# The head of a fused conv and gate kernel: the first superblock's scatters moved ahead of most loads of the second, scatters shared out anew between SP and POOL, one eviction on VectorE, one block's order, six more zero matmuls

## The chip, the core and the metric

The kernel runs on one core of a Trainium2 chip. The metric is the time that the device takes for one execution, in microseconds (us), as the median over runs.

## What is computed

Two stages on x of shape (8, 4224, 192), cut to what matters. First a causal convolution over time with 7 taps, whose taps are a softmax per head (8 heads of 24 channels); then a gated projection.

```python
w = softmax(weight, axis=-1)                    # (8 heads, 7 taps)
a[b, s, h, :] = sum_k w[h, k] * x_pad[b, s + k, h, :]
gate_pre[b, s, :] = sum_k conv_w[k, :] * a_pad[b, s + k, :]   # 5 taps
gate = sigmoid(gate_pre)
out = (gate * (a @ w_val)) @ w_out              # both 192 x 192
```

All of it is float32.

## The kernel before

**Layout.** The eight sequences lie as two streams of four, back to back, with padding between. The streams are cut into 14 *superblocks*; superblock g has NJS[g] windows of 122 tokens for each of 5 strips of a head (2, 3, 3, 3, then 5). The 192 channels fill one and a half times 128 partitions, so a superblock of `a` is held as x1 (128 partitions: heads 0 to 4 and a third of head 5, both streams beside each other) and x2 (the other 64 channels, one stream on each half of the partitions).

**First stage.** The convolution of the first stage is a matmul (line 312): 128 tokens of a window on the partitions, 120 columns (5 strips x 24 channels) as the stationary operand, and a 128 x 122 band matrix made of the softmax weights as the moving one. Four such matmuls fill a PSUM tile `pc_u`; that is a *unit* u. Superblock 0 has units 0 to 3, superblock 1 units 4 to 9, superblock 2 units 10 to 15, superblock 3 units 16 to 21. Heads come in the order 6, 7, 5, 0, 1, 2, 3, 4 (QUADS). In float32 each matmul stands as two records in the profile. ScalarE copies the unit's PSUM tile to SBUF (line 321, tile `e`). When all windows of a head are copied, `scatter` (lines 333 to 363) issues DMAs that move its rows from `e` to their partitions in x1 or x2: one DMA for heads 0 to 4, two for heads 6 and 7, four for head 5. These DMAs are issued by SP, except that in superblocks 0 to 2 heads 5, 6 and 7 are issued by POOL (but two of head 5's DMAs in superblock 0), and heads 3 and 4 of superblock 0 by ScalarE.

**Loads.** x arrives by DMAs from SP, `x_i` (line 161), with two heads in each for superblocks 0 to 3: x_0 to x_3 are superblock 0, x_4 to x_7 superblock 1, x_8 to x_11 superblock 2. There are eight buffers. Six loads and the weights (`wv`, `wo`) are issued at the start (lines 188 to 192); the later ones are issued from `conv_unit` once a load's last head has been scattered, up to the number that `allowed` (line 143) gives. SP's queue is in order: a scatter that waits for its eviction holds up each load behind it.

**Second stage.** It runs over *blocks* n, two for superblocks 0 to 3 (blocks 0 and 1 are superblock 0). For the 5-tap gate, ScalarE opens an accumulator in PSUM (`pa` for the x1 part, `pb` for x2, line 384), VectorE adds the other four taps (line 391) and ScalarE closes it with a sigmoid into g1 or g2 (line 404). The projection splits each float32 operand into two parts, h rounded by ScalarE (lines 412, 420) and l = x - h by POOL (lines 413, 421), and makes three matmuls of each product (`diagonal`, `main`, `rows`, lines 447 to 470); a smaller piece goes in plain float32 (`columns`, line 485). The 192 output channels come as three chunks, 0 and 1 (the two streams of the first 128) and 2. VectorE multiplies value and gate (line 504, into g), the product is split again and projected with w_out, ScalarE copies the result out (line 520) and SP stores it (line 525).

**Order.** No scheduler reorders anything: each engine executes in the order in which the code is written. The prologue (lines 548 to 569) decodes the weights on VectorE, does the units 0 to 9 and opens blocks 0 and 1; the loop at line 571 does blocks 0 to 3, the loop at line 604 the rest. WARM (line 94) are counts of matmuls on zeros (line 204), which compute nothing that is used: 11 ahead of unit 0, 5 ahead of unit 4, 14 ahead of unit 7.

In the profile's rows and below, buffer numbers are left out where a group is meant: `x<-xw` is a load, `x<-e` a scatter, `pc<-band,x` a unit's matmul, `pw<-zero` a zero matmul.

Of the kernel before, what the change touches and what calls it, by code (L numbers as in the profile page):

```python
# [22 lines left out]
M = NS * HC  # L23
# [69 lines left out]
BY_POOL, EARLY, AHEAD = 3, 4, 6  # L93
WARM = 11, 5, 14

# [6 lines left out]
def kernel(  # L102
# [40 lines left out]
    def allowed(i):  # L143
        g = loads[i][0]
        a, b = first_load[g], first_load[g + 1]
        if g == 0:
            return b + 2 if i < b - 1 else first_load[2]
        if g == 1:
            return b + (0, 2, 2, 4)[i - a]
        if g < EARLY:  # L150
            return b + (first_load[g + 2] - b) * (i + 1 - a) // (b - a)
        return i + 1 + AHEAD
# [34 lines left out]

    load_x(3)
    load_raw("wv")
    load_x(4)  # L190
    load_raw("wo")
    load_x(6)

# [104 lines left out]
    def conv_unit(u):  # L298
# [21 lines left out]
        w = len(ws) * WIN  # L320
        nc.scalar.copy(e[:, a : a + w], pc[:M, :w])  # L321
        done = [hi for hi, j in ws if j == n - 1]
        for hi in done:
            h = QUADS[q][hi]
            i, at = home[g, h]
            last = at == len(loads[i][1]) - 1
            if last and g >= BY_POOL:
# [5 lines left out]
    def scatter(g, h, e):  # L333
# [3 lines left out]
        x1, x2 = x1s[g], x2s[g]  # L337
        if g < BY_POOL and h >= 5:
            dma = nc.gpsimd.dma_start
        elif g == 0 and h in (3, 4):  # L340
            dma = nc.scalar.dma_start
        else:
            dma = nc.sync.dma_start
# [10 lines left out]
        else:  # L354
# [4 lines left out]
            for i, (a, b) in enumerate(ends):  # L359
                if h == 5:  # L360
                    send(x2[64 * i + 48 : 64 * i + 64], 8, HC, a, b, nc.sync.dma_start if g == 0 else dma)
                else:
                    send(x2[64 * i + h - 6 : 64 * i + 48 : 2], 0, HC, a, b)
# [126 lines left out]
    def split(n):  # L490
        if n >= N:
            return
        x1, x2 = views(n)
        if n == 0:
            xs[n, 2] = split2(sp, "x", n, x2)
        xs[n, 1] = split1(sp, "x", n, x1)
        if n > 0:
            xs[n, 2] = split2(sp, "x", n, x2)
# [48 lines left out]

    nc.scalar.activation(warm2, rs[:, 0:1], AF.Sigmoid)
    w_val.decode()
    w_val.join(nc.vector)  # L550
    put(cwt.rearrange("p a k -> p (a k)"), w_val.pr, 0, 128, 2 * D, 2 * D + 2 * KG)
    conv(first_unit[1])
    w_val.cast(nc.gpsimd)
# [17 lines left out]
    for n in range(HEAD):  # L571
        k = 2 if n < 2 else 3
        diagonal("v", n)
        split(n + 1)
        diagonal("o", n - 1)
        main("v", n, 0)
        main("v", n, 1)
        gate_taps(n + 1, 0, 1, k)
        columns("v", n)
# [143 lines left out]
```

## Time and profile before

| what | value |
|---|---|
| median of 3 runs | 390.54 us (390.15 to 391.44) |
| the profiled execution | 393.35 us, of which its span 391.6 us |
| TensorE busy | 378.0 us (97%) |
| VectorE busy | 342.3 us (87%) |
| ScalarE busy | 323.8 us (83%) |
| GpSimd busy | 254.8 us (65%) |
| DMA | 82.49 MB, 211 GB/s on average |
| granted TensorE clock, mean | 0.991 |

Times in the profile count from the start of the span. PE is TensorE, PEld its weight load, DVE is VectorE, ACT is ScalarE, POOL is GpSimd, SP is SyncE; a q behind a name is that engine's DMA queue, where the row's duration is that of the issue and not of the transfer. A row of the timeline gives the start, the duration from the first to the last of a merged group, the instruction, and in brackets the idle time of the engine just before it with what ended it. The chain of waits is followed back from the last instruction, at each step to what released it. A row of the stretches gives busy time and count for PE, PEld, DVE, ACT and POOL, then the granted clock, the share of the 16 DMA engines that was busy, and GB/s.

### The profile page before, as it was taken

How to read it: one execution, taken by the hardware profiler on the slowest of the kernel's cores; microseconds unless marked ns; L12 is line 12 of the kernel's file. 1: busy time of each engine (PE TensorE's matmuls, PEld its weight loads, DVE VectorE, ACT ScalarE, POOL GpSimd, SP SyncE). 2: the span in 40 equal slices, each digit the busy share in tenths (PEclk: the TensorE clock that was granted, in tenths of full speed). 3: DMA queues.
4: the chain of work that ended last, by engine and by line, in shares of the span. 5: the costliest groups of instructions: out<-in, count | busy, mean ns of one | idle time of the engine just before them, and what ended most of it. 6: DMA issues, size and time to landing. Idle time of an engine off the chain costs nothing.

```text
span 391.6 us, 8620 instructions
## 1 busy us (share of the span) xinstructions
PE 378.0 (97%) x3204; PEld 321.6 (82%) x3204; DVE 342.3 (87%) x424; ACT 323.8 (83%) x525; POOL 254.8 (65%) x177
## 2 busy tenths in 40 slices
PE   8699999999999999999999999999999999999895
PEld 8687988898888888888888888888888787788684
DVE  4669899888998998998999899899899999999970
ACT  7458888988888888888889988888888888887863
POOL 1959765566667665666665666766566676776871
PEclk9969999999999999999999999999999999999999
DMA  8777869998687689778868868758987644333223
GB/s 293 210 195 223 253 214 290 258 239 272 210 251 216 180 260 256 210 217 253 224 194 256 219 185 261 218 178 253 257 226 227 211 160 146 114 135 133 80 106 144
DMA packets 38209, 82.49 MB, mean 211 GB/s; under 512 B 4856, under 2 KB 17528, under 8 KB 38168
## 3 DMA queue, kind: packets, MB, share of 16 engines
q1 hardware_dynamic: 36720, 79.90, 67.6%
q0 software_dynamic: 896, 1.31, 1.4%
q10 hardware_dynamic: 552, 0.73, 0.6%
q8 instruction: 25, 0.41, 0.5%
q14 instruction: 16, 0.13, 0.1%
HBM read 29.34 MB, written 26.00 MB: 141 GB/s over the span
## 4 chain that ended last, share of the span: by engine, by line
PE 72%; DVE 13%; DMA 5%; ACT 4%; issue 3%; SPq 2%; POOL 0%; DVEq 0%; ACTq 0%
PE pc L312 20%; PE o L457 10%; PE v L457 9%; PE v L485 7%; PE v L470 6%; PE o L485 6%; DVE pa L391 6%; PE o L470 5%; PE o L447 5%; PE v L447 4%; DVE pb L391 4%; DVE g L504 3%; DMA x<-e 2%; DMA x<-xw 2%; DMA scr<-wv 1%
## 5 line engine op out<-in xcount | busy, mean ns | idle before, releaser
L391 DVE SCALAR_TENSOR_TENSOR pa<-x,cwt,pa 128x1004 f32<-128x1004 f32 (+5 forms) x144 | 172.9, 1201 | 10.7 <-ACT pa L384 6.8
L413 POOL TENSOR_TENSOR xl<-x,xh 128x1004 fp32r<-128x1004 f32 (+5 forms) x36 | 74.8, 2077 | 73.1 <-ACT xh L412 58.9
L312 PEld LDWEIGHTS pc<-band,x 128*120 128x120 f32 x912 | 103.1, 187 | 7.1 <-issue 3.9
L312 PE MATMUL pc<-band,x 128*120 128x122 f32 x912 | 104.2, 272 | 4.3 <-DMA x<-xw 3.8
L391 DVE SCALAR_TENSOR_TENSOR pb<-x,cwt,pb 128x502 f32<-128x502 f32 (+5 forms) x144 | 102.2, 710 | 3.8
L413 POOL TENSOR_TENSOR pl<-g,ph 128x1004 fp32r<-128x1004 f32 (+5 forms) x36 | 79.4, 2204 | 10.3 <-ACT ph L412 7.7
L504 DVE TENSOR_TENSOR g<-v,g 128x502 f32<-128x502 f32 (+5 forms) x108 | 65.8, 642 | 21.1 <-PE v L470 16.1
L404 ACT ACTIVATE g<-pa 128x1004 f32<-128x1004 f32 (+5 forms) x36 | 34.5, 959 | 38.8 <-DVE pa L391 21.1
L321 ACT COPY e<-pc 120x488 f32<-120x488 f32 x114 | 59.1, 586 | 6.4 <-PE pc L312 6.3
L421 POOL TENSOR_TENSOR pl<-g,ph 128x502 fp32r<-128x502 f32 (+5 forms) x36 | 43.0, 1194 | 32.8 <-ACT ph L420 32.7
L520 ACT COPY ot<-o 128x502 f32<-128x502 f32 (+5 forms) x108 | 56.2, 551 | 3.3 <-PE o L457 2.6
L421 POOL TENSOR_TENSOR xl<-x,xh 128x502 fp32r<-128x502 f32 (+5 forms) x36 | 41.8, 1162 | 0.0
L384 ACT ACTIVATE pa<-x,cwt 128x1004 f32<-128x1004 f32 (+5 forms) x36 | 37.8, 1051 | 4.8 <-DMA x<-e 3.7
L485 PEld LDWEIGHTS v<-x,wvf 128*64 128x64 f32 x576 | 29.1, 136 | 11.8 <-issue 11.4
L485 PE MATMUL v<-x,wvf 128*64 128x125 f32 (+4 forms) x576 | 37.2, 270 | 0.0
L412 ACT CAST ph<-g 128x1004 fp32r<-128x1004 f32 (+5 forms) x36 | 35.1, 976 | 1.5 <-DVE g L504 1.5
L485 PE MATMUL o<-g,wof 128*64 128x125 f32 (+4 forms) x576 | 35.6, 264 | 0.0
L412 ACT CAST xh<-x 128x1004 fp32r<-128x1004 f32 (+5 forms) x36 | 34.6, 961 | 0.0
L485 PEld LDWEIGHTS o<-g,wof 128*64 128x64 f32 x576 | 30.9, 136 | 0.1
L457 PE MATMUL o<-ph,woh 128*128 128x502 f32 (+5 forms) x72 | 30.9, 429 | 0.0
L457 PE MATMUL v<-xh,wvh 128*128 128x502 f32 (+5 forms) x72 | 27.2, 377 | 0.3 <-ACT e L321 0.3
L457 PE MATMUL v<-xh,wvl 128*128 128x502 f32 (+5 forms) x72 | 27.1, 377 | 0.0
(75 smaller groups left out, 573.1 us busy)
## 6 DMA issues: line engine op xcount, KB each, us to landing
x<-xw SPq DMA_DIRECT2D x64, 300.0 KB
out<-ot SPq DMA_DIRECT2D x24, 753.0 KB
x<-e SPq DMA_DIRECT2D x40, 285.9 KB
x<-xw SPq DMA_DIRECT2D x20, 360.0 KB
out<-ot SPq DMA_DIRECT2D x8, 672.0 KB
x<-e SPq DMA_DIRECT2D x32, 141.6 KB
x<-e SPq DMA_DIRECT2D x25, 171.6 KB
x<-e SPq DMA_DIRECT2D x16, 94.4 KB
```

The source lines that it names most:

```text
L312: nc.tensor.matmul(pc[:M, k * WIN : (k + 1) * WIN], lhsT=xtiles[i][:, c : c + M], rhs=band[:, 4 * q + hi, :], start=True, stop=True,)
L321: nc.scalar.copy(e[:, a : a + w], pc[:M, :w])
L384: nc.scalar.mul(acc, views(n, 0)[i], cwt[:, i, 0:1])
L391: nc.vector.scalar_tensor_tensor(out=acc, in0=views(n, k)[i], scalar=cwt[:, i, k : k + 1], in1=acc, op0=ALU.mult, op1=ALU.add,)
L412: nc.scalar.copy(h, x)
L413: nc.gpsimd.tensor_tensor(out=l, in0=x, in1=h.bitcast(F32), op=ALU.subtract)
L421: nc.gpsimd.tensor_tensor(out=l, in0=x, in1=h.bitcast(F32), op=ALU.subtract)
L457: nc.tensor.matmul(acc, lhsT=a[:, r], rhs=b[:, q], start=(fresh and i == 0), stop=(not fresh and i == 2))
L470: nc.tensor.matmul(acc, lhsT=a[p, r], rhs=b[p], start=(fresh and i == 0), stop=(not fresh and i == 2))
L485: nc.tensor.matmul(acc[p, c], lhsT=w.f[:, W12 : W12 + 64], rhs=x[:, q, c], start=False, stop=(i == 3),)
L504: nc.vector.tensor_tensor(out=v, in0=banks.pop(("v", n, q)), in1=v, op=ALU.mult)
L520: nc.scalar.copy(ots[n][:, q * m : (q + 1) * m], banks.pop(("o", n, q)))
```

## The change

Seven things are changed, all in the head (superblocks 0 to 2):

1. The load x_3 is issued ahead of `wv`.
2. Load x_5 is no longer issued at the start, but behind the scatter of head 0 of superblock 0; x_6 and x_7 are issued behind the scatter of head 6 of superblock 1, which waits for the eviction of pc_4, and no longer behind the scatters of superblock 0.
3. The table FROM_POOL now says which heads POOL scatters: of superblock 0 heads 5, 6, 7 and, new, head 2; of superblock 1 heads 5 and 7, and no longer head 6; of superblock 2 none. SP issues the rest, and in superblock 1 also the two DMAs of head 5's rows in x2.
4. Unit 0 is evicted by VectorE instead of ScalarE, and unit 0 is written ahead of the decoding of w_val, so that VectorE has the copy ahead of that decoding.
5. In block 1 ScalarE and POOL split the x2 part (chunk 2) ahead of the x1 part.
6. In block 1 TensorE does the `diagonal` of the output projection of block 0 behind `main` of the values and no longer ahead of it.
7. 20 zero matmuls stand ahead of unit 7 instead of 14.

SP's queue in the head, before, from the fourth load to the loads of superblock 2 (x_i are loads with their numbers, scr the raw weights, x1_g and x2_g the rows of superblock g, e_g_q the evicted heads; the last number of each name only tells tiles apart):

```order
L186 DMA scr_2_101<-wv 128x788
L161 DMA x_3_105<-xw 128x480
L186 DMA scr_1_100<-wo 128x768
L161 DMA x_4_108<-xw 128x720
L161 DMA x_5_110<-xw 128x720
L350 DMA x2_0_177<-e_0_0_178 16x5x122 x2
L350 DMA x1_0_176<-e_0_0_178 24x5x244
L350 DMA x1_0_176<-e_0_1_200 24x5x244 x2
L161 DMA x_6_217<-xw 128x720
L161 DMA x_7_219<-xw 128x720
L350 DMA x1_1_236<-e_1_0_238 24x5x366
L161 DMA x_8_266<-xw 128x720
```

And the same stretch of SP's queue in the changed kernel:

```order
L188 DMA scr_2_101<-wv 128x788
L188 DMA scr_1_100<-wo 128x768
L163 DMA x_4_108<-xw 128x720
L354 DMA x2_0_164<-e_0_0_165 16x5x122 x2
L354 DMA x1_0_163<-e_0_0_165 24x5x244
L163 DMA x_5_198<-xw 128x720
L354 DMA x1_0_163<-e_0_1_200 24x5x244
L354 DMA x2_1_233<-e_1_0_234 24x5x180 x2
L163 DMA x_6_243<-xw 128x720
L163 DMA x_7_245<-xw 128x720
L354 DMA x2_1_233<-e_1_0_234 16x5x180 x2
L354 DMA x1_1_232<-e_1_0_234 24x5x366
```

Load x_5 has moved from ahead of three scatter issues to behind them, one scatter of superblock 0 has gone to POOL, two scatters of superblock 1 now stand ahead of x_6 and x_7, and x_8 stands behind two more (its row follows the last one shown).

TensorE before, from unit 4 to unit 7 (pc_u is unit u, pw the zero matmuls):

```order
L312 MATMUL pc_4_239<-band_91,x_4_108 120x122 x4
L312 MATMUL pc_5_247<-band_91,x_4_108 120x122 x2
L312 MATMUL pc_5_247<-band_91,x_5_110 120x122 x2
L312 MATMUL pc_6_255<-band_91,x_5_110 120x122 x4
L204 MATMUL pw_270<-zero_114 120x122 x14
L312 MATMUL pc_7_305<-band_91,x_6_217 120x122 x4
```

And in the changed kernel:

```order
L313 MATMUL pc_4_235<-band_91,x_4_108 120x122 x4
L313 MATMUL pc_5_247<-band_91,x_4_108 120x122 x2
L313 MATMUL pc_5_247<-band_91,x_5_198 120x122 x2
L313 MATMUL pc_6_255<-band_91,x_5_198 120x122 x4
L205 MATMUL pw_270<-zero_112 120x122 x20
L313 MATMUL pc_7_311<-band_91,x_6_243 120x122 x4
```

The order there is the same; six zero matmuls are added, six matmuls (pc_4 and half of pc_5) need x_4 alone, the six behind them x_5.

SP's queue for superblock 2 before, with the loads around it:

```order
L161 DMA x_10_327<-xw 128x720
L161 DMA x_11_329<-xw 128x720
L161 DMA x_12_410<-xw 128x720
L350 DMA x1_2_387<-e_2_0_389 24x5x366
L161 DMA x_13_423<-xw 128x720
```

And in the changed kernel:

```order
L163 DMA x_10_333<-xw 128x720
L163 DMA x_11_335<-xw 128x720
L354 DMA x2_2_394<-e_2_0_395 24x5x180 x4
L163 DMA x_12_416<-xw 128x720
L354 DMA x1_2_393<-e_2_0_395 8x5x180 x2
L354 DMA x2_2_394<-e_2_0_395 16x5x180 x2
L354 DMA x1_2_393<-e_2_0_395 24x5x366
L163 DMA x_13_429<-xw 128x720
```

Eight scatters that POOL issued now stand on SP, four of them ahead of x_12 and all of them ahead of x_13.

The diff:

```diff
--- before.py
+++ after.py
@@ -91,7 +91,9 @@
 XW = max(PER_LOAD[n] * n * M for n in NJS)
 LAG = 2
 BY_POOL, EARLY, AHEAD = 3, 4, 6
-WARM = 11, 5, 14
+
+FROM_POOL = {(0, 2), (0, 5), (0, 6), (0, 7), (1, 5), (1, 7)}
+WARM = 11, 5, 20
 
 HEAD = 4
 
@@ -144,7 +146,7 @@
         g = loads[i][0]
         a, b = first_load[g], first_load[g + 1]
         if g == 0:
-            return b + 2 if i < b - 1 else first_load[2]
+            return b + min(i + 1, 2)
         if g == 1:
             return b + (0, 2, 2, 4)[i - a]
         if g < EARLY:
@@ -185,11 +187,10 @@
     def load_raw(name):
         nc.sync.dma_start(raw[name][1], raw[name][2])
 
-    load_x(3)
+    load_x(4)
     load_raw("wv")
-    load_x(4)
     load_raw("wo")
-    load_x(6)
+    load_x(5)
 
     one = cp.tile([128, 1], F32, name="one")
     nc.vector.memset(one, 1.0)
@@ -318,12 +319,15 @@
             )
         a = (ws[0][0] * n + ws[0][1]) * WIN
         w = len(ws) * WIN
-        nc.scalar.copy(e[:, a : a + w], pc[:M, :w])
+        if u == 0:
+            nc.vector.tensor_copy(e[:, a : a + w], pc[:M, :w])
+        else:
+            nc.scalar.copy(e[:, a : a + w], pc[:M, :w])
         done = [hi for hi, j in ws if j == n - 1]
         for hi in done:
             h = QUADS[q][hi]
             i, at = home[g, h]
-            last = at == len(loads[i][1]) - 1
+            last = at == len(loads[i][1]) - 1 or (g, h) == (1, QUADS[0][0])
             if last and g >= BY_POOL:
                 load_x(allowed(i))
             scatter(g, h, e[:, hi * n * WIN : (hi + 1) * n * WIN])
@@ -335,7 +339,7 @@
         r = n * WIN
         hf = half(n)
         x1, x2 = x1s[g], x2s[g]
-        if g < BY_POOL and h >= 5:
+        if (g, h) in FROM_POOL:
             dma = nc.gpsimd.dma_start
         elif g == 0 and h in (3, 4):
             dma = nc.scalar.dma_start
@@ -358,7 +362,7 @@
                     send(x1[120:128, i * second(n) :], 0, 8, a, b)
             for i, (a, b) in enumerate(ends):
                 if h == 5:
-                    send(x2[64 * i + 48 : 64 * i + 64], 8, HC, a, b, nc.sync.dma_start if g == 0 else dma)
+                    send(x2[64 * i + 48 : 64 * i + 64], 8, HC, a, b, nc.sync.dma_start if g < 2 else dma)
                 else:
                     send(x2[64 * i + h - 6 : 64 * i + 48 : 2], 0, HC, a, b)
 
@@ -491,10 +495,10 @@
         if n >= N:
             return
         x1, x2 = views(n)
-        if n == 0:
+        if n < 2:
             xs[n, 2] = split2(sp, "x", n, x2)
         xs[n, 1] = split1(sp, "x", n, x1)
-        if n > 0:
+        if n >= 2:
             xs[n, 2] = split2(sp, "x", n, x2)
 
     def gated(n, q):
@@ -546,10 +550,11 @@
             todo[a + i * (b - a) // k] += 1
 
     nc.scalar.activation(warm2, rs[:, 0:1], AF.Sigmoid)
+    conv(1)
     w_val.decode()
     w_val.join(nc.vector)
     put(cwt.rearrange("p a k -> p (a k)"), w_val.pr, 0, 128, 2 * D, 2 * D + 2 * KG)
-    conv(first_unit[1])
+    conv(first_unit[1] - 1)
     w_val.cast(nc.gpsimd)
     w_out.decode()
     zeros(WARM[1])
@@ -572,9 +577,12 @@
         k = 2 if n < 2 else 3
         diagonal("v", n)
         split(n + 1)
-        diagonal("o", n - 1)
+        if n != 1:
+            diagonal("o", n - 1)
         main("v", n, 0)
         main("v", n, 1)
+        if n == 1:
+            diagonal("o", n - 1)
         gate_taps(n + 1, 0, 1, k)
         columns("v", n)
         gated(n, 2)
```

## The prediction

> **What bounds the kernel now.** I read the page first, then the chain of waits, then the first 40 us stretch by stretch, since the order of instructions differs only there (the first three superblocks). From the page: busy time by engine, and the chain by engine.
>
> ```profile
> PE 378.0 (97%) x3204; PEld 321.6 (82%) x3204; DVE 342.3 (87%) x424; ACT 323.8 (83%) x525; POOL 254.8 (65%) x177
> PE 72%; DVE 13%; DMA 5%; ACT 4%; issue 3%; SPq 2%; POOL 0%; DVEq 0%; ACTq 0%
> ```
>
> TensorE is busy 378.0 of 391.6 us, and the chain is 72% its work. What it loses in the head can be seen in the chain there.
>
> ```profile
> 10.70 0.89 SPq L350
> ...
> 14.35 5.89 DMA x<-xw
> 20.23 0.14 issue
> 20.37 5.22 PE pc L312 x24
> 25.59 0.02 issue
> 25.61 0.57 ACT e L321
> ...
> 28.05 0.33 ACT g L404
> 28.38 0.02 issue
> 28.40 1.24 DVE g L504 x3
> ```
>
> Read downwards: SP issues scatters; behind them in its queue stands load x_6, issued at 14.35 and landed 5.89 us later; TensorE then does pc_7 to pc_9; the last eviction, at 25.61, lets ScalarE close block 0's gates (the last from 28.05) and that releases, at 28.40, VectorE's first products. So the change is worth what it moves the end of pc_9, now 25.59, less what is lost again before 38 us.
>
> The stretches show why those matmuls are dear (after the engines' busy times come PEclk, DMA share, GB/s).
>
> ```profile
> 8.00:10.00 2.00, 2.00 (x21) 2.00 (x20) 1.90 (x6) 1.83 (x5) 0.88 (x2) 1.00 1.01 404
> 10.00:12.00 2.00, 2.00 (x21) 2.00 (x20) 1.89 (x7) 0.57 (x1) 2.00 (x4) 1.00 0.61 175
> 12.00:14.00 2.00, 2.00 (x21) 2.00 (x20) 1.88 (x6) 0.69 (x2) 1.19 (x3) 1.00 0.68 161
> 18.00:20.00 2.00, 0.00 (x0) 0.00 (x0) 1.14 (x2) 1.98 (x4) 1.98 (x5) 0.84 1.00 308
> 20.00:22.00 2.00, 1.63 (x8) 1.66 (x9) 1.93 (x3) 0.20 (x1) 2.00 (x2) 0.50 1.08 248
> 26.00:28.00 2.00, 2.00 (x26) 1.74 (x26) 0.40 (x1) 1.97 (x5) 0.00 (x0) 0.95 0.49 140
> ```
>
> And TensorE and ScalarE there, from the timeline, with the spread of landing times of all transfers of x tiles in the first 60 us.
>
> ```profile
> 6.45 3.62 PE L312 MATMUL pc<-band,x 128*120 128x122 f32 x32 [0.51 <-DVE band L229]
> 10.96 2.69 PE L312 MATMUL pc<-band,x 128*120 128x122 f32 x24
> 13.48 3.10 PE L204 MATMUL pw<-zero 128*120 128x122 f32 x28
> 20.37 5.21 PE L312 MATMUL pc<-band,x 128*120 128x122 f32 x24 [3.78 <-DMA x<-xw]
> 8.27 1.57 ACT L321 COPY e<-pc 120x488 f32<-120x488 f32 x3
> 9.31 4.99 SPq L350 DMA_DIRECT2D x<-e  x5
> 13.78 1.50 ACT L321 COPY e<-pc 120x488 f32<-120x488 f32 x3
> DMA to landing us min/median/max: 2.2/4.4/8.7
> ```
>
> Each matmul stands as two records: 12 matmuls x24. The zero matmuls end at 13.48 + 3.10 = 16.58, TensorE is idle 3.78 us, and the clock is halved within 18 to 20 (0.84 = full for 68% of it, so from 19.36, 2.8 us into the gap) and full again from about 26.2 (0.95 in 26 to 28), 5.8 us after work resumed. The same 24 records that take 2.69 us at full clock take 5.21. The stall is thus 3.8 us of waiting and 2.5 us of slow clock.
>
> **The change, part by part.** *Loads and scatters on SP.* VectorE evicts pc_0 while ScalarE does pc_1, once its matmuls are done (halfway through 3.62 from 6.45, about 8.3 to 8.4). The copy ends at about 9.0 instead of 9.3, so SP starts its scatters at 9.05, not 9.31: 0.26 earlier. Three scatters take it from 9.31 to 10.70 + 0.89 = 11.59 today, 2.28 us; load x_5, so far among the first loads, is now issued behind them, at 11.35. Its landing is the largest unknown: 2.2 to 8.7 us, median 4.4. The DMA share from 10 to 14 us is 0.61 to 0.68, against 1.00 and 1.08 from 18 to 22, when x_6 was under way, so I take 3.6, below the median: x_5 at 15.0.
>
> *TensorE.* pc_4 and the first two matmuls of pc_5 need only x_4: half of 2.69 from about 11.05, to 12.4. Then a gap that before doesn't have, 12.4 to 15.0: 2.6 us. It is just shorter than the 2.8 after which the clock fell, so I take full clock. The rest of pc_5 and pc_6 is 1.35; twenty zero matmuls are 3.10 / 14 x 20 = 4.43, of which six new ones 1.33. They end at 15.0 + 1.35 + 4.43 = 20.8.
>
> *x_6.* Its issue now waits for the eviction of pc_4, which is the first copy of the group at 13.78 and ends at about 14.35, and for the two scatters of head 6 (0.76 each by the three above): 15.9. Landing between 4.4 (median) and 5.89 (its own, with the scatters of four heads just ahead); I take 5.0: 20.9. The zeros meet it, TensorE never idles there, and pc_7 to pc_9 take 2.69: end at 23.55 instead of 25.59, a gain of 2.05.
>
> By the row above, the gap may not outlast 2.8 us. The Trainium skill, "TensorE: Matmul & The Clock Gate", section "What's actually happening", says that a free-running window of about 3.4 us decides, and that one idle window returns the clock to half. The trace agrees only in kind: 0.84 and then 0.50 follow 3.78 us of idling, the fall at 2.8. By the row the clock is safe if x_5 lands before 15.2, by the page before 15.8; at my 15.0 the sum is 2.05 by both, at 15.75 (the median) it would be 1.37 by the page and a loss by the row, which is the first rival.
>
> *Small edits, costed at nothing.* Rows that bear on them:
>
> ```profile
> 6.88 0.67 DVE L229 TENSOR_TENSOR band<-band,rs 128x488 f32<-128x488 f32 x1 [0.48 <-ACT band L221]
> 7.77 0.37 DVE L242 TENSOR_SCALAR scr<-scr 128x394 int32<-128x394 int32 x1 [0.23 <-DMA scr<-wv]
> 10.71 2.50 ACTq L350 DMA_DIRECT2D x<-e  x2
> 13.31 0.56 ACT L282 CAST wvh<-wvf 128x448 fp32r<-128x448 f32 x1 [2.63 <-DVE scr L246]
> 18.02 0.77 ACT L384 ACTIVATE pa<-x,cwt 128x608 f32<-128x608 f32 x1 [2.75 <-DMA x<-e]
> 22.27 2.26 DVE L391 SCALAR_TENSOR_TENSOR pb<-x,cwt,pb 128x304 f32<-128x304 f32 x4
> ```
>
> VectorE's copy isn't in the trace. ScalarE's takes 0.57; VectorE's products from PSUM, 304 wide, take 1.24 / 3 = 0.41, or 0.66 at 488: I take 0.6. It starts at 7.55 and ends at 8.2, where the decoding of w_val starts at 7.77 now. That decoding is late anyway: x_3 ahead of wv adds 128 x 480 x 4 B, 246 KB, which is 0.6 us at the 404 GB/s of 8 to 10 us. So wvf comes 0.7 later; ScalarE's cast of it at 13.31 stands behind DMA issues that end at 10.71 + 2.50 = 13.2, which hides it (without that cover: 0.7 on pc_4's eviction and on x_6). Head 2's scatter goes from SP to POOL, whose seventh issue it becomes. pa_0 opens when the last row of x1 lands, 18.02 now; it now also stands behind the eviction of pc_6 (16.35 + 0.6), so 17 to 18. VectorE's taps of block 0 end at 22.27 + 2.26 = 24.5, before the gate closing that would move from 28.05 to 26.0. So the gain of 2.05 reaches the products at 28.40.
>
> *Block 1 and superblock 2.* The rows:
>
> ```profile
> 31.93 0.40 PE L447 MATMUL v<-xl,wvh 128*128 128x302 f32 x1 [0.46 <-POOL xl L421]
> 32.08 2.25 DVE L391 SCALAR_TENSOR_TENSOR pb<-x,cwt,pb 128x302 f32<-128x302 f32 x4
> 34.59 1.16 DVE L391 SCALAR_TENSOR_TENSOR pa<-x,cwt,pa 128x896 f32<-128x896 f32 x1 [0.26 <-issue]
> 35.65 1.23 DVE L504 TENSOR_TENSOR g<-v,g 128x302 f32<-128x302 f32 x3
> 33.14 0.47 SPq L161 DMA_DIRECT2D x<-xw  x1
> 37.72 5.20 PE L312 MATMUL pc<-band,x 128*120 128x122 f32 x48
> 35.35 3.49 POOL L350 DMA_DIRECT2D x<-e  x6
> ```
>
> Chunk 2 first takes away the 0.46 that TensorE waits for xl of chunk 2. But from 28.40 to 36.9 VectorE is the late one: its products, taps and products follow each other with 0.26 between them, and the chain runs there. So I count 0, at most 0.46.
>
> The eight scatters of superblock 2 leave POOL (3.49 for six, 0.58 each) and stand on SP ahead of x_13, issued at 33.14 now: 33.14 - 2.05 + 8 x 0.6 = 35.9, landed at 40.3 by the median. TensorE needs x_13 at the nineteenth of the 24 matmuls from 37.72: 41.6, or 39.6 with the gain. That is 0.7 late by the median, nothing if it lands in 3.7 us; I take back 0.5. POOL's freed time buys nothing, since no row above waits for its later work.
>
> Sum: -2.05 + 0.5 = -1.55. The profiled execution took 393.35 us, its span is 391.6, so the span becomes 390.05; the median of the runs, 390.54, is 2.8 below the profiled execution, and 390.54 - 1.5 = 389.0 is the forecast.
>
> **The rivals.** *The new gap halves the clock (slower).* If x_5 lands in 4.4 us, at 15.75, the gap is 3.35 us, longer than the 2.8 that the row above needed; from 15.2 on it decides. At half clock for 5.8 us after resuming, as in before, TensorE does 2.9 us less. Between x_5's landing and the end of pc_9 stand 1.35 + 4.43 + 2.69 = 8.47, so pc_9 ends at 15.75 + 8.47 + 2.9 = 27.1, which is 1.55 late: 392.1; half of that slow time would give 390.6. For it: the median, and the scatters in the same queues. Against it: the half-empty DMA share from 10 to 14.
>
> *The gain is given back.* x_8, x_9 and x_13 all stand further back in SP's queue; if TensorE or ScalarE waits 1.5 us more for them than I take, 2.05 shrinks to nearly nothing: 390.3. For it: the landing times up to 8.7. Against it: the DMA share falls to 0.49 by 26 to 28, so there is room.
>
> *More than forecast.* x_6 lands in the median 4.4, x_13 in time and the 0.46 counts: 2.05 + 0.45, so 388.0. Against it: the zeros end only at 20.8.
>
> *Loads late, clock kept:* x_5 lands at 16.5 with a lucky phase, pc_9 ends at 25.0, less 0.5: 390.5.
>
> **How the numbers follow.** Chances: forecast 0.42 (own range 387.6 to 389.6), more than forecast 0.09, halved clock 0.27, given back 0.14, loads late 0.08. About 0.3%, 1.2 us, is what a measurement here can tell from no change: below 389.4 is faster, above 391.7 slower. Faster: 0.40 + 0.09 and 0.01 of the given-back case, 0.50. Slower: 0.20 of the halved clock, 0.03 of the late loads, 0.23. The same: 0.27. The range runs from 387.3 (a gain of 2.5 and an x_5 that lands faster still) to 392.3 (just over the halved clock's price); outside is less than 2 in 10.
>
> **What would show it.** Right: pc_5 resumes by about 15 us, the granted clock is 1.00 from 6 us on, pc_7 starts near 20.9, VectorE's first products start near 26.3, and the conv matmuls of superblock 2 run through. Wrong: a granted clock of 0.5 between 14 and 23 us, with the zero matmuls taking twice 0.22 us each; x_5 landing after 16; an idle gap of TensorE ahead of pc_17; or the first products no earlier than 28 us.

## The result and the profile after

The forecast was 389.0, faster. The changed kernel is slower, and outside the range.

| | before | after |
|---|---|---|
| median, us (lowest to highest, 6 runs) | 390.35 (389.77 to 391.44) | 395.55 (393.98 to 397.11) |
| profiled execution, us (span) | 393.35 (391.6) | 395.47 (393.7) |
| x_6 landed / pc_9 done | 20.24 / 25.59 | 19.90 / 26.33 |
| first products g | 28.40 | 29.14 |

The ratio is 1.0118, 95% interval [1.0093, 1.0143]: about 4.6 us lost, and 5.2 between the two medians. A few executions of the kernels below took 520 to 979 us; the ratios leave them out, and for the two kernels whose profiled execution was one of them (a_sb2_pool, b_sb2_sp) the trace read is that of a further single execution, called a look. In the profiled execution everything happens in the first 45 us again. The chain of waits of the changed kernel in the head:

```profile
8.94 0.70 SPq L354
...
10.31 0.89 SPq L354
...
11.26 5.12 DMA x<-xw
...
16.42 2.22 PE pc L313 x12
18.64 5.15 PE pw L205 x40
23.79 2.54 PE pc L313 x24
...
29.14 1.24 DVE g L508 x3
```

The load on the chain is now x_5, not x_6: issued where the prediction had it (11.26 for 11.35), but 5.12 us on its way instead of 3.6. Then forty records of zero matmuls stand on the chain, where before they filled a wait. TensorE's timeline, and the stretches (engines' busy times, then PEclk, DMA share, GB/s):

```profile
16.42 2.22 PE L313 MATMUL pc<-band,x 128*120 128x122 f32 x12 [4.12 <-DMA x<-xw]
23.63 2.69 PE L313 MATMUL pc<-band,x 128*120 128x122 f32 x24
36.91 0.40 PE L474 MATMUL o<-ph,woh 64*128 64x304 f32 x1 [1.28 <-DVE g L508]
38.46 3.94 PE L313 MATMUL pc<-band,x 128*120 128x122 f32 x36
44.07 1.52 PE L313 MATMUL pc<-band,x 128*120 128x122 f32 x12 [1.66 <-DMA x<-xw]
```

```profile
12.00:14.00 2.00, 0.30 (x3) 0.12 (x2) 1.90 (x8) 1.03 (x2) 1.56 (x3) 1.00 0.86 201
14.00:16.00 2.00, 0.00 (x0) 0.00 (x0) 1.92 (x3) 0.00 (x0) 0.96 (x1) 1.00 0.73 233
16.00:18.00 2.00, 1.58 (x10) 1.58 (x11) 0.36 (x1) 0.57 (x1) 0.00 (x0) 0.77 0.95 255
18.00:20.00 2.00, 2.00 (x12) 2.00 (x11) 0.05 (x1) 1.32 (x3) 2.00 (x4) 0.50 0.99 324
20.00:22.00 2.00, 2.00 (x19) 2.00 (x18) 1.93 (x3) 1.32 (x3) 1.64 (x3) 0.88 0.73 151
```

The wait of 3.78 ahead of unit 7 has become one of 4.12 in the middle of unit 5, and the granted clock falls as it did in before: in the trace's record it is half from 17.07 to 20.48. The zeros, in part at that clock, run to 23.79, 3.0 later than forecast, though all of x_6 was there at 19.90. Of these 3.0 us, 1.4 are the late x_5 (work resumes at 16.42 for 15.0); in the other 1.6 the rest of unit 5, unit 6 and the zeros take 7.37 us for the 5.78 of the forecast. SP's queue, where x_13 is the load at 39.67:

```profile
11.26 0.48 SPq L163 DMA_DIRECT2D x<-xw  x1
...
31.45 3.84 SPq L354 DMA_DIRECT2D x<-e  x4
35.39 0.47 SPq L163 DMA_DIRECT2D x<-xw  x1
35.91 3.66 SPq L354 DMA_DIRECT2D x<-e  x5
39.67 0.45 SPq L163 DMA_DIRECT2D x<-xw  x1
```

Superblock 2's scatters cost SP 0.96 each in the first four and 0.73 in the next five, not the 0.6 taken. x_13 is issued 3.8 later than forecast, of which 2.8 are the head's own lateness (38.46 for 35.67 at the start of the superblock's conv), and TensorE waits 1.66 for it in the middle of that conv.

Between the two profiled executions: pc_9 ends 0.74 later, block 2's first output copy starts 2.66 later (59.68 for 57.02), block 32's 2.63, and the spans differ by 2.1. That is not the 4.6 of the ratio. The rest lies in the profile of before, which the first experiment takes up.

### The profile page after: what moved, and what is told of

Same layout as the page of the kernel before. It is cut to its first block, busy times and chain, and to the rows that moved or that the text cites. A ratio compares the mean times of both kernels' runs of the same rounds, so it can differ in the third digit from the quotient of the medians.

```text
span 393.7 us, 8634 instructions
## 1 busy us (share of the span) xinstructions
PE 378.4 (96%) x3216; PEld 322.3 (82%) x3216; DVE 343.1 (87%) x425; ACT 323.8 (82%) x524; POOL 248.4 (63%) x166
## 4 chain that ended last, share of the span: by engine, by line
PE 86%; DVE 4%; issue 3%; DMA 2%; ACT 2%; POOL 1%; SPq 1%; DVEq 0%; POOLq 0%
PE pc L313 21%; PE o L461 13%; PE v L461 11%; PE v L489 8%; PE v L474 7%; PE o L489 7%; PE o L474 7%; PE o L451 5%; PE v L451 5%; PE pw L205 3%; DMA x<-xw 2%; DVE pa L395 2%; DVE g L508 1%; DVE pb L395 1%; ACT e L325 1%
## 5 line engine op out<-in xcount | busy, mean ns | idle before, releaser
L313 PEld LDWEIGHTS pc<-band,x 128*120 128x120 f32 x912 | 101.9, 185 | 8.8 <-DMA x<-xw 6.2
L461 PE MATMUL v<-xl,wvh 128*128 128x502 f32 (+5 forms) x72 | 27.2, 377 | 0.1
```

The costliest lines, as they stand in the source:

```text
L313: nc.tensor.matmul(pc[:M, k * WIN : (k + 1) * WIN], lhsT=xtiles[i][:, c : c + M], rhs=band[:, 4 * q + hi, :], start=True, stop=True,)
L461: nc.tensor.matmul(acc, lhsT=a[:, r], rhs=b[:, q], start=(fresh and i == 0), stop=(not fresh and i == 2))
```

## The experiments

Block landmarks serve as a ruler: the start of ScalarE's first output copy of a block, as the difference to the same in the unchanged kernel run again (b_copy, block 0 at 35.86, block 2 at 55.85, block 34 at 380.95; minus is earlier). "Half clock" lists where the trace of the kernel's profiled execution has the granted clock at a half between 6 and 385 us. Each ratio is against executions of before in the same session (medians 390.13 to 390.63).

| kernel | median | ratio [95%] | block 0 / 2 / 34 | half clock from (length) |
|---|---|---|---|---|
| before | 390.35 | | +1.18 / +1.17 / +1.14 | 19.36 (6.83) |
| after | 395.55 | 1.0118 [1.0093, 1.0143] | +1.98 / +3.82 / +3.77 | 17.07 (3.41) |
| after_look, one execution | 397.42 | | +2.63 / +4.21 / +5.67 | 14.98 (6.83), 38.87, 373.38 (3.41 each) |
| b_copy | 390.20 | 0.9998 [0.9974, 1.0022] | 0 | 19.95 (3.41) |
| b_loads | 392.71 | 1.0043 [1.0025, 1.0062] | +0.09 / +0.08 / +0.06 | 16.62 (3.41) |
| b_sb2_sp | 392.63 | 1.0060 [1.0032, 1.0089] | -1.21 / +0.29 / +0.48 (first look) | 34.55 (3.41) |
| b_sb2_sp_look2, one execution | 390.79 | | -1.55 / -1.04 / -1.11 | none |
| b_z28 | 390.83 | 0.9999 [0.9977, 1.0021] | -2.05 / -2.15 / -1.71 | none |
| a_x5_early | 394.14 | 1.0097 [1.0061, 1.0133] | +1.25 / +2.65 / +2.63 | 22.64 (3.41) |
| a_sb2_pool | 394.71 | 1.0104 [1.0071, 1.0137] | +2.47 / +4.03 / +4.03 (look) | 14.33 (6.83), 38.22 (3.41) |
| a_no_zeros | 394.08 | 1.0108 [1.0073, 1.0142] | +0.45 / +1.90 / +1.84 | 15.03 (10.24) |
| a_loads | 393.36 | 1.0072 [1.0042, 1.0102] | +0.05 / +1.32 / +1.26 | 24.85 (3.41) |
| a_loads_sb2 | 392.75 | 1.0043 [1.0015, 1.0070] | -1.79 / -1.90 / -0.43 | 366.69 (3.41) |
| a_x5_sb2 | 393.16 | 1.0060 [1.0037, 1.0084] | +0.05 / -0.01 / +1.51 | 20.38, 368.54 (3.41 each) |
| a_ls_z14 | 393.35 | 1.0053 [1.0026, 1.0080] | -0.90 / +0.67 / +2.64 | 34.95, 369.46 (3.41 each) |
| a_ls_b1 | 392.75 | 1.0051 [1.0025, 1.0077] | -0.67 / -0.71 / +0.86 | 368.68 (3.41) |
| a_ls_tail | 392.21 | 1.0030 [1.0008, 1.0053] | -1.02 / -1.07 / -1.02 | none |
| a_b1_tail | 391.40 | 1.0028 [1.0010, 1.0045] | -1.86 / -1.88 / -1.87 | none |

Between block 2 and block 32 nothing moves by more than 0.5 us in any of them: the kernel's body carries the head's shift rigidly.

**b_copy: the kernel before, unchanged.**

> The kernel before once more, unchanged, for its span and its granted clock in several executions. The profiled execution of before took 393.35 us, the median of its other runs 390.35. Theory A: that execution is untypical, because the 3.78 us gap ahead of unit 7 cost it the clock for 6.8 us (2.5 us of slow matmuls), and most executions keep the clock: spans near 388.5 us at a mean clock near 0.999, now and then 391 to 392 at 0.99. Theory B: the profiled execution is typical and the 2.8 us are what profiling adds: spans near 391.6 at 0.991 each time.

```profile
13.36 3.10 PE L204 MATMUL pw<-zero 128*120 128x122 f32 x28
20.06 4.35 PE L312 MATMUL pc<-band,x 128*120 128x122 f32 x24 [3.60 <-DMA x<-xw]
...
30.76 0.40 PE L447 MATMUL v<-xl,wvh 128*128 128x302 f32 x1 [0.73 <-POOL xl L421]
...
35.00 0.40 PE L470 MATMUL o<-ph,woh 64*128 64x304 f32 x1 [0.25 <-DVE g L504]
```

The same kernel, 1.2 us earlier at every landmark: work resumes 0.31 earlier, and the clock was at half for one stretch of 3.41, not for 6.83 (pc_7 to pc_9 take 4.35 for 5.21). The mean granted clock of each execution tells the rest: of 35 further executions of before, 11 had 0.997 or more, with spans of 387.3 to 388.5 (median 388.2); the median of the other 24 is 389.75. In the other sessions 10 of 17, 13 of 32 and 12 of 23 had it. One stretch of 3.41 at half takes 0.0044 off the mean, so 0.997 leaves no room for one. So before keeps its clock in a third to three fifths of its executions, and the profiled one, at 391.6, was among those that lost most. The 2.8 us that the prediction set aside as the difference between profile and median were largely that lost clock, as far as these executions tell; none that keeps it was traced.

**b_loads: before, with only the new order of loads.**

```diff
-            return b + 2 if i < b - 1 else first_load[2]
+            return b + min(i + 1, 2)
-    load_x(6)
+    load_x(5)
-            last = at == len(loads[i][1]) - 1
+            last = at == len(loads[i][1]) - 1 or (g, h) == (1, QUADS[0][0])
```

> The kernel before with the changed order of loads alone: x_5 behind head 0's scatter, x_6 and x_7 at the place behind head 6 of superblock 1 (whose scatter POOL still issues, so that SP needn't wait for pc_4). Theory A (a late x_5 is a loss by itself): x_5 lands near 16, units 5 and 6 end near 17.7, 14 zero matmuls end at 21 to 22, unit 9 ends near 24 to 25: 1.5 to 2.5 us slower than the kernel before, near 392. Rival C (x_5 and x_6 only change places, and the end of unit 9 is set by x_6 in both): within 0.7 us of the kernel before.

```profile
15.85 2.10 PE L312 MATMUL pc<-band,x 128*120 128x122 f32 x12 [3.57 <-DMA x<-xw]
17.75 4.21 PE L204 MATMUL pw<-zero 128*120 128x122 f32 x28
21.80 2.69 PE L312 MATMUL pc<-band,x 128*120 128x122 f32 x24
```

Its profile stands level with b_copy's, which lost the clock too. But here every one of 12 executions has a mean clock of 0.990 to 0.994, as with one or two lost stretches each time. So the new order takes away the executions that keep the clock. It may cost more than that: the profiled execution, with a span of 390.2, is among the shortest of the 12, whose median is 390.9, where before's eleven at 0.990 to 0.994 in the same session have 390.1. Together it is 0.43%.

**a_loads: the changed kernel, with the old order of loads** (the three lines above, undone).

> The changed kernel, with loads x_5, x_6 and x_7 where they stood before: x_5 at the start, x_6 and x_7 behind the scatters of superblock 0. Everything else as changed, with the 20 zero matmuls and superblock 2 on SP. With x_5 alone undone, the wait ahead of unit 5 went and new ones of 1.4 and 0.7 us came ahead of units 7 and 8, since x_6 still stands behind two scatters that wait for pc_4. Theory A (the order of the loads as a whole is the main loss): x_6 is issued near 13 and lands near 18 to 19, unit 9 ends near 21.5 to 22.5, 2 us earlier than in the kernel before; the wait for x_13, 1.2 to 1.7 us, stays: near 390, the same as before. Rival B (SP's longer queue is the main loss): near 393 to 394. Rival E (the DMA traffic decides and not the order of issue; x_6 lands at 20 or later whatever stands ahead): near 392.

0.72% instead of 1.18%, with intervals that just overlap: a step of the size of b_loads, from the other side. The gap is gone (0.81 for x_5), but the clock falls at 24.85 behind three waits for xh and xl of 0.24, 0.37 and 0.75, and x_13 is still waited for, 1.07.

**a_x5_early: the changed kernel, with x_5 among the first loads.**

```diff
-    load_x(5)
+    load_x(6)
```

> The changed kernel, with load x_5 issued at the start again, right behind x_4; all else as changed. In the changed kernel x_5 landed at 16.4 us, units 5 and 6 waited 4.1 us for it, and the end of unit 9 came at 26.3. Theory A (the late x_5 is the main loss): the wait ahead of unit 5 is gone, the 20 zero matmuls end near 18.5, unit 7 starts when x_6 lands, near 20 to 21, at full clock, and ends near 23.5: 2.8 us less than the changed kernel, about 392.7. Rival B (the loss is superblock 2 on SP): no change, 395.5. Rival C (x_6 then lands later by as much, since x_5 merely changes places with it): under 1 us less.

The gap ahead of unit 5 shrinks to 1.00, but TensorE waits 1.44 for x_6 and 0.71 for x_7 and the clock falls at 22.64. With x_6 still behind the scatters, x_5 or x_6 is late, whichever is first.

**a_no_zeros: the changed kernel, without the zero matmuls ahead of unit 7.**

```diff
-WARM = 11, 5, 20
+WARM = 11, 5, 0
```

> The changed kernel without the 20 zero matmuls ahead of unit 7; all else as changed. In the changed kernel x_6 had landed at 19.9 us while zero matmuls ran until 23.8. Theory A (with x_5 late, the zeros run past the landing of x_6 and are themselves the delay): unit 7 starts near 20, unit 9 ends near 23 to 24 instead of 26.3, 2.5 to 3.5 us less than the changed kernel, about 392.5. Rival (the zeros keep the clock up and pay for themselves): the clock stays at half for 6.8 us or more, units 7 to 9 take 5.2 us, and the time is within 1 us of the changed kernel's 395.5.

```profile
16.19 2.80 PE L313 MATMUL pc<-band,x 128*120 128x122 f32 x12 [4.33 <-DMA x<-xw]
19.60 5.21 PE L313 MATMUL pc<-band,x 128*120 128x122 f32 x24 [0.61 <-ACT e L325]
```

pc_7 starts 4.0 earlier, but pc_9 is done only 1.5 earlier (24.8): without the zeros the clock stays at half to 25.27, so pc_7 to pc_9 take 5.21. The zeros buy back 2.5 of the 4.0 us that they cost.

**a_sb2_pool and a_sb2_pool_look: the changed kernel, with superblock 2's scatters on POOL.**

```diff
-FROM_POOL = {(0, 2), (0, 5), (0, 6), (0, 7), (1, 5), (1, 7)}
+FROM_POOL = {(0, 2), (0, 5), (0, 6), (0, 7), (1, 5), (1, 7), (2, 5), (2, 6), (2, 7)}
```

> The changed kernel, with the eight scatters of superblock 2 (heads 5, 6 and 7) issued by POOL again; all else as changed. In the changed kernel x_13 was issued at 39.7 and landed at 44.1, and TensorE waited 1.7 us for it ahead of unit 17. Theory A: that wait goes, 1.7 us less than the changed kernel, about 393.8, and the late x_5 and the zero matmuls stay. Rival B (the SP queue in superblock 2 and behind it is the main loss): back to the kernel before, about 390.5. Rival D (POOL's splits come later again and give it back): no change.

> The changed kernel with superblock 2's scatters on POOL, for a look at its trace (timed, it took 394.71, 1.0104). No wait for x_13, and block 2 no later against block 0 than in the unchanged kernel; the 4 us gap ahead of unit 5 and the end of pc_9 near 26.3 as in the changed kernel. If both hold, the time that it doesn't win back is lost by the granted clock elsewhere, and the page shows where.

The time, 1.0104, does not differ measurably from the 1.0118 of the changed kernel. In the look, no wait for x_13, and the same gap of 4.12. Yet block 2 is 1.56 later against block 0 as if x_13 had been late: behind a wait of 1.30 for g in block 1 the clock falls at 38.22. So the expectation that block 2 would not be late is wrong. What removes the wait for x_13 does not remove its price.

**after_look: the changed kernel, a second execution.**

> A second execution of the changed kernel. If the first was typical: a gap of 3.5 to 4.5 us ahead of unit 5, a half-clock window that begins in it or within 1 us behind it, zero matmuls that run 3 us or more past the landing of x_6, and a wait of 1 to 2 us for x_13; 394 to 397. If the late x_5 was an accident of the first execution: x_5 lands before 15 us, no half-clock window, and a time below 392.

```profile
36.00:38.00 2.00, 0.71 (x10) 0.47 (x6) 2.00 (x4) 1.91 (x4) 0.15 (x1) 1.00 0.77 212
38.00:40.00 2.00, 2.00 (x13) 1.83 (x12) 1.97 (x3) 1.72 (x5) 2.00 (x2) 0.72 0.38 110
40.00:42.00 2.00, 2.00 (x12) 2.00 (x12) 1.96 (x3) 0.80 (x2) 1.83 (x2) 0.50 0.73 202
```

397.42, with a gap of 3.97 for x_5, and the clock at half from 14.98 for 6.83 instead of 3.41. This time the wait for g in block 1 (1.29, as against 1.28 in the first execution) does cost the clock, from 38.87; with TensorE that slow x_13 is in time. Block 2 is 1.58 later against block 0, in the first execution 1.84. A third fall comes at 373.38, behind a wait of 1.36 for g.

**b_sb2_sp, and two looks: before, with superblock 2's scatters on SP alone.**

```diff
-        if g < BY_POOL and h >= 5:
+        if g < 2 and h >= 5:
```

> The kernel before with one part of the change: the eight scatters of superblock 2 issued by SP instead of by POOL. Theory A (that part alone costs what the landmarks of the other runs say, 1.3 to 1.8 us between blocks 0 and 2): TensorE waits 1.2 us or more for x_13 inside the conv matmuls of superblock 2, the head is as in the unchanged kernel up to there, and the median is 391.5 to 392.2, ratio 1.003 to 1.005. Theory B (x_13 is late only because everything ahead of it on SP is late in the changed kernel): no wait for x_13 over 0.5 us, and the same time within 0.2%. A half-clock window behind the wait (46% idle was enough elsewhere) would add up to 1.7 to A.

> The kernel before with superblock 2's scatters on SP alone, for a look at its trace (timed, it took 392.63, 1.006). If x_13 is late by itself, TensorE waits 1.2 us or more for it inside the 24 conv matmuls of superblock 2 and block 2 starts that much later against block 0; if there is no such wait, the 2 us are lost elsewhere and the reading of the landmarks is wrong.

> A second look at the kernel before with superblock 2's scatters on SP alone; the first had no wait for x_13, but a wait of 1.33 for g and a half-clock window behind it. Theory A (x_13 is late only where everything ahead of it on SP is late): no wait for x_13 over 0.3 us again if unit 7 starts before 19.5 us, and one of 0.5 to 1.8 if it starts after 20. Theory B (the scatters never delay x_13 here): no such wait in either case, and block 2 is later against block 0 only if a half-clock window lies between them.

TensorE in the first look, ahead of unit 7 and in block 1, and a stretch behind that:

```profile
18.96 3.03 PE L312 MATMUL pc<-band,x 128*120 128x122 f32 x24 [2.29 <-DMA x<-xw]
...
33.68 0.41 PE L470 MATMUL o<-ph,woh 64*128 64x304 f32 x1 [1.33 <-DVE g L504]
```

```profile
34.00:36.00 2.00, 2.00 (x13) 1.82 (x10) 1.97 (x4) 1.46 (x4) 1.99 (x1) 0.64 0.40 101
```

x_13 is not late by itself: issued at 35.16 and 34.75 in the looks, not at 39.67, it is waited for 0 and 0.35 us (0.3 was the most expected). The 0.6% comes another way. Relieved of the scatters, POOL delivers xl in time, so the wait of 0.73 for xl that b_copy has in block 1 is gone; VectorE is no earlier for it, and the wait for g is 1.33 and 1.44 instead of 0.25. Behind the first the clock fell (34.55), and block 2 lost 1.50 us; behind the second it did not, and block 2 lost 0.51. My forecast that VectorE is the late one there was right, and so POOL's and TensorE's earlier work bought nothing. What it did not see: two short waits that become one long one can cost the clock. The looks also suggest why before keeps its clock at times: x_6 is waited for 2.29 and 1.85 here and the clock holds; at 3.60 and 3.78, in the two traces of before, it falls.

**a_loads_sb2: the changed kernel, with the old order of loads and superblock 2 on POOL.**

> The changed kernel, with the loads x_5 to x_7 where they stood before and the eight scatters of superblock 2 on POOL again. Left of the change are head 2 on POOL, heads 6 and part of 5 of superblock 1 on SP, the eviction by VectorE, the order in block 1 and the 20 zero matmuls. Theory A: both waits are gone and the better clock stays: 1.2 to 1.7 us less than with the loads undone alone, near 388.5, less than the kernel before by 1 to 2 us. Rival D (what is left of the change is neutral): 390.2, the same as before.

Both suspects undone, 0.43% remains, though in the profile the head is 1.9 us ahead of b_copy up to block 32. Then 1.5 of it go at once: TensorE's wait near the end, and the stretches around it.

```profile
366.18 0.47 PE L474 MATMUL o<-ph,woh 64*128 64x448 f32 x1 [1.58 <-DVE g L508]
```

```profile
364.00:366.00 2.00, 0.59 (x5) 0.20 (x3) 1.97 (x3) 0.29 (x1) 2.00 (x2) 1.00 0.05 21
366.00:368.00 2.00, 1.82 (x7) 1.26 (x8) 1.96 (x5) 1.97 (x4) 1.07 (x2) 0.67 0.00 0
368.00:370.00 2.00, 2.00 (x6) 1.70 (x6) 1.93 (x3) 1.70 (x4) 1.81 (x2) 0.50 0.00 0
```

The unchanged kernel (b_copy) at the same place, with the same instructions in the same order:

```profile
363.14 0.47 PE L447 MATMUL o<-pl,woh 128*128 128x448 f32 x1 [0.56 <-POOL pl L421]
...
368.11 0.47 PE L470 MATMUL o<-ph,woh 64*128 64x448 f32 x1 [0.56 <-DVE g L504]
```

The same pattern again: 0.56 and 0.56 have become 1.58, VectorE's time there is the same, and the clock falls. Every kernel built on the changed one has this wait, from 1.36 to 1.59 (but for the two below that fill it); every one built on before has two shorter ones, none over 1.08.

**a_x5_sb2: a_x5_early with superblock 2 on POOL.**

> The changed kernel with x_5 among the first loads and superblock 2's scatters on POOL, everything else as changed (x_6 and x_7 stay where the change put them). Theory A (two separate losses, the late x_5 and the late x_13, and a remainder of the other edits): no wait for x_13, median near 392.7, ratio about 1.005, as with all loads put back. Theory B (x_6 and x_7 behind the scatters cost as much as x_5 did): waits for x_6 and x_7 of 0.7 to 1.5 us with a half-clock window, median 393.5, ratio 1.008.

No wait for x_13, none of block 2's lateness; x_6 is waited for 2.23 and the clock falls there and again behind the wait near the end.

**a_ls_z14 and a_ls_b1: a_loads_sb2 with fourteen zero matmuls, and with block 1's order as before.**

```diff
-WARM = 11, 5, 20
+WARM = 11, 5, 14
```
```diff
-        if n < 2:
+        if n == 0:
             xs[n, 2] = split2(sp, "x", n, x2)
...
-        if n != 1:
-            diagonal("o", n - 1)
+        diagonal("o", n - 1)
...
-        if n == 1:
-            diagonal("o", n - 1)
```

> The changed kernel with the loads as before, superblock 2 on POOL and fourteen zero matmuls ahead of unit 7 instead of twenty. With twenty it took 392.75 (1.0043). Theory A (the six zeros are the remainder): 390.4 to 391.2, ratio at most 1.002. Theory B (the remainder is lost behind unit 7, in waits for xl, x_8 and g, which the end of the zeros does not set): unchanged, 392 to 393, and pc_7 either starts 1.3 earlier or waits for x_6 instead.

> The changed kernel with the loads as before, superblock 2 on POOL, and block 1's order as before (chunk 2 split second, out diagonals of block 0 ahead of block 1's main products). Theory A (block 1's order is the remainder: the last out tap of block 0 waits 1.54 for VectorE's g, where the kernel before waits 0.25): that wait falls to about 0.3 to 0.5, but block 2 starts no earlier than VectorE lets it, so the gain is at most 1.2: 391.5 to 392.0. Theory B (VectorE sets the end of the head whatever the order of TensorE): the wait moves or shrinks, block 2 starts at the same time within 0.3, median unchanged at 392.7, and what remains is clock windows lost elsewhere.

Neither changes the median measurably, so neither the six zeros nor block 1's order is shown to be the remainder by itself. The old order does what was expected of it: the wait for g in block 1 is 0.40 instead of 1.54, with 1.10 for xl ahead of it, and no fall of the clock between them.

**a_ls_tail and a_b1_tail: a_loads_sb2 and a_ls_b1 with six zero matmuls in the wait near the end.** They add zero to a bank that TensorE holds at that point.

```diff
+                if (what, n, i) == ("o", 32, 0) and acc is two[0]:
+                    for _ in range(6):
+                        nc.tensor.matmul(
+                            acc[:M, :WIN], lhsT=zero[:, :M], rhs=zero[:, M:], start=False, stop=False
+                        )
```

> The changed kernel with the loads as before, superblock 2 on POOL, and six zero matmuls (1.3 us, adding zero to a bank that is already held) in the 1.5 us for which TensorE waits for VectorE's g near 366 us. Without them it took 392.75 (1.0043), and the half-clock window behind that wait, in this kernel's profile and in three of its kin, cost block 34 1.5 us. Theory A (that window is the remainder): no half-clock window between 360 and 375, block 34 as far ahead of the unchanged kernel's profile as block 32, more executions at a granted clock of 0.997 or above than the 2 of 12, median 391.2 to 392.0, ratio 1.001 to 1.003. Theory B (the remainder is lost in the head, in some executions by clock windows behind the waits for x_7, x_8 and g): the tail window goes, but the median stays within 0.3 of 392.75.

> The same six zero matmuls, and block 1's order as before too, so that the wait of 1.54 for g at 33 us is 0.4 as it was with that order. Theory A (two waits of 1.5, each of which loses the clock in part of the executions): median 390.2 to 391.2, ratio at most 1.002, most executions at a clock of 0.997 or above. Theory B (as with a_ls_tail, the losses are in the waits for xl and x_7 that remain): 392 to 392.8, and executions below 0.994 stay frequent.

The stretches of a_ls_tail around the filled wait:

```profile
365.00:367.00 2.00, 2.00 (x19) 1.62 (x15) 1.97 (x4) 0.37 (x1) 2.00 (x2) 1.00 0.01 3
367.00:369.00 2.00, 2.00 (x12) 1.52 (x11) 1.97 (x5) 1.97 (x4) 1.23 (x2) 1.00 0.00 0
```

The fall is gone, and block 34 keeps the lead of block 32 in both. Of 12 executions of a_ls_tail, 7 have a mean clock of 0.997 or more, of a_loads_sb2 2. Median 392.21 and 391.40, neither as low as expected (at most 392.0 and 391.2), and the intervals overlap with those of their bases. By the clocks, the wait near the end is part of the remainder; the medians do not show it, and it is not all of it: a_b1_tail is still 0.28% above before, with spans from 387.9 to 390.7 at 0.997 or more, where before, in 12 such executions beside it, has 387.7 to 389.9. Where these executions lose time without losing the clock I have not found.

**b_z28: before, with twenty-eight zero matmuls ahead of unit 7.** It was to beat both by filling the wait for x_6.

```diff
-WARM = 11, 5, 14
+WARM = 11, 5, 28
```

> The kernel before with 28 zero matmuls ahead of unit 7 instead of 14, nothing else. They would end near 19.6 us, just ahead of x_6, which lands at 20.1 to 20.2. Theory A (half of before's executions lose the clock in the 3.6 us gap ahead of unit 7: spans of 387.0 to 388.0 at a mean clock of 0.997 or more, 390.1 to 391.6 at 0.994 or less): the gap closes, every execution keeps its clock, the spread shrinks to about 1 us, and the median falls from 390.1 to about 389. Rival (the clock goes elsewhere, in the first zeros or at the end): median and spread as before.

11 of 12 executions keep the clock, and the profile's head is 2.15 ahead of b_copy's, but the median is 390.83: at full clock its spans have a median of 388.8 (387.7 to 389.7), which lies between before's 388.2 in the executions that keep the clock and 389.75 in the others. By that, zeros that outlast a short wait cost about what they save where the wait is long. No kernel here beats before.

## Why the prediction was wrong, point by point

- *SP's first scatter at 9.05, x_5 issued at 11.35*: 8.94 and 11.26. Right, and so was VectorE's copy (0.67 at 7.51 for 0.6 at 7.55).
- *x_5 lands 3.6 later, at 15.0*: 5.12, at 16.38. **This is the step that failed first.** The argument was a DMA share of 0.61 to 0.68 between 10 and 14 us. In the changed kernel it is 0.52 to 12 and 0.86 and 0.73 to 16, never full, and x_5 still took 5.12, in after_look 5.2 (issued at 10.63, used at 15.89). In b_loads it took 4.3 (11.52 to 15.81). All three land after the 15.2 that the first rival needed. A share with room left said nothing on how soon one transfer lands; the median of 4.4 was the better guess, though it mixes loads with scatters. Before's own loads of this size just before and behind, x_4 to x_6, took 6.1, 6.0 and 5.9 by the semaphore updates in its trace, none of them near 3.6.
- *New gap 2.6, full clock kept*: 4.12, half clock for 3.41. Of the 1.5 us more, 1.4 are the late x_5 and 0.1 that pc_5's matmuls wait from 12.3 on. The first rival had the mechanism, and the mean clocks of all executions of the changed kernel (0.980 to 0.995) and of b_loads fit it; I gave it 0.27. Its condition was too mild: 2.8 us was how far into before's gap the clock fell, not what a gap needs. A wait of 2.23 lost the clock in a_x5_sb2, so the gap of 2.6 in the forecast was not safe either. The Trainium skill, "TensorE: Matmul & The Clock Gate", section "What's actually happening", put the price nearer than my row in this execution: it gives a window of about 3.4 us, and the half-clock stretch was 3.41, where I took 5.8 from before. In after_look it was 6.83.
- *The zeros end at 20.8 and meet x_6*: they ended at 23.79, x_6 was there at 19.90. Work of fixed length, added to cover a wait, is itself late when what stands ahead of it is late. a_no_zeros shows that it still pays for 2.5 of its 4.0 us through the clock.
- *pc_9 ends at 23.55, and the gain reaches the products*: 26.33 and 29.14. The second half is right: from the end of pc_9 to the products it is 2.81 us in both kernels.
- *x_13 0.7 late, 0.5 taken back*: 1.66. The size was off, since a scatter on SP costs 0.96 and 0.73 there and not 0.6: against the start of the conv x_13 is issued 1.0 later than forecast, and the wait is 1.0 longer. The runs showed more: with x_13 in time (a_sb2_pool_look, after_look) block 2 was as late through a lost clock.
- *Chunk 2 first, POOL's freed time: nothing, VectorE is the late one*: VectorE was, from 29.14 to 36.38 in 7.24 us as from 27.23 to 34.48 in 7.25 in b_copy. The step that failed is "nothing": the merged wait of 1.26 to 1.54 for g loses the clock in 4 of the 11 profiles that have it at 1.26 or more, at about 1.5 us each, and in none of the six in which two shorter waits stand there (the last section says more of the other seven).
- *Profiled execution 2.8 above the median, taken off the sum as it is*: it hid that before keeps its clock in a third to three fifths of its executions. The gain of 2.05 was counted against an execution that had lost the clock for 6.83 us. In one that keeps it, with x_6 waited for 2.29 (b_sb2_sp_look), pc_9 is done by 22.0, which is earlier than the 23.55 of the forecast: in such an execution there was nothing of that gain to win.

By the experiments on before, the new order of loads alone costs 0.43% and superblock 2's scatters on SP alone 0.60%; undoing both leaves 0.43% of 1.18%. The parts do not simply add up: undone in the changed kernel, superblock 2's scatters alone give back only 0.14 points. Of the 0.43%, the merged wait near the end is a part by the clocks alone. Why the last scatter is early enough for that merge in the changed kernels is open: b_copy issues its last three from 353.91 and ScalarE still waits for them until 360.27; a_loads_sb2 issues them from 351.98, and they no longer hold up ScalarE at 357.33, with nothing changed in the order of either queue there. The share of the other small edits was not tried one by one.

## What to carry to other kernels

Before costing a change, look at how the time of the unchanged kernel spreads over its executions, and cost against the typical one: a wait that is long in the profile may be short in the median. How soon a transfer lands is read from like transfers in like places, not from a DMA share that has room left. And the sum of TensorE's waits is not the whole price: removing a short wait ahead of an engine that is late anyway only lengthens the next wait, and one wait of 1.5 us may cost the clock where two of 0.6 do not.

## What the runs showed of the hardware

The granted clock falls and recovers in steps of 3.41 us: 17.07 and 20.48; 38.87, 42.29 and, further on, 373.38 and 376.79 in after_look. All falls of one execution lie on one grid: in after_look 38.87 is 7 steps of 3.413 behind 14.98, and 373.38 is 98 steps behind 38.87; it is so in each trace with several falls. In the Trainium skill, "TensorE: Matmul & The Clock Gate", section "What's actually happening", the window of about 3.4 us is the same, and the trace agrees. But the page has the clock fall after an idle window, and here a window with a single wait of 1.3 to 1.6 us in it, under half of 3.41, was enough in 4 profiles in block 1 and in 5 near the end; the measurement decides.

It is not a threshold on the length of the wait: 2.29 kept the clock in b_sb2_sp_look, 2.23 lost it in a_x5_sb2, and all of 3.57 or more lost it. How the wait lies on the grid explains a part. A boundary of the grid, found by counting back from a later fall, cuts the 2.29 into windows in which TensorE is busy for 2.61 and 1.92, so idle for 0.80 and 1.50:

```profile
14.07:17.48 3.41, 2.61 (x25) 2.42 (x24) 1.46 (x2) 1.46 (x4) 3.41 (x5) 1.00 0.92 274
17.48:20.90 3.42, 1.92 (x16) 1.77 (x17) 2.92 (x4) 2.33 (x5) 3.40 (x7) 1.00 1.00 253
```

In a_x5_sb2 the 2.23 lie in one window, and the clock falls at its end:

```profile
16.97:20.38 3.41, 1.18 (x12) 1.03 (x11) 3.30 (x5) 1.19 (x3) 3.09 (x4) 1.00 0.95 264
```

Of the eleven merged waits in block 1, four are cut in this way, with at most 1.06 of the wait in one window (a_loads_sb2, a_x5_sb2, a_ls_tail, b_sb2_sp_look2), and all four kept the clock; the seven in one window kept it at 1.26, 1.28 and 1.30 and lost it at 1.29, 1.30, 1.33 and 1.44. Over all traces, behind 6 us, each window at full clock with 1.92 us or more of idle time was followed by a fall and none with under 1.29 was. Between the two the idle time does not decide: 1.85 kept the clock in b_sb2_sp_look2, and of the ten waits near the end, all in one window, the five that lost it have 1.36 to 1.58 and the five that kept it 1.43 to 1.59. This stays open.
